# A planned attention and mixture kernel whose instruction order comes from a fixed list instead of a list scheduler, with its last product in two halves

## The chip, the cores and the metric

The kernel runs on one core of one Trainium2 chip. The metric is the time of one execution in microseconds (us), as the median of several runs. The engines are TensorE (PE in the profile; PEld is its weight load), VectorE (DVE), ScalarE (ACT), GpSimd (POOL), and SyncE (SP), which issues the transfers. Each engine takes its own instructions in the order in which the program emits them, and waits at semaphores for the others.

## The reference

```python
# attention over 4 x 8 heads: x is 512 x 64, state is 32 x 64 for each head
scores = scale * x @ state.T;   a  = exp(scores - max);  a  /= a.sum;   xread = a @ state
scores2 = scale * state @ x.T;  a2 = exp(scores2 - max); a2 /= a2.sum;  sread = a2 @ x
x = concat([xread, sread], axis=2)           # as 2176 tokens x 512
# mixture 1: 512 -> 2048 -> 512
h = x @ w_in;  g = h * tanh(softplus(h));  x = g @ w_out
# mixture 2: 512 -> 1536 -> 512, gated
xn = x / sqrt(mean(x * x) + 1e-6) * rms_g
g = xn @ w_gate;  out = (silu(g) * (xn @ w_val)) @ w_out2
```

All arrays are float32.

## The kernel before

**The work.** The tokens are cut into chunks c (512 tokens each, and a last one of the 128 rows of `sread`), the hidden width of each mixture into units u of 512. A float32 product is made of three float16 products (high by high, high by low, low by high parts), so TensorE runs nothing but short float16 matmuls in the mixtures, and VectorE and ScalarE make the two parts of every operand ("split" steps: `hi`, `l`, `s`, `join` for the weights, then `sh`, `sl`). The second mixture and the later products use seven block products in place of eight (`S1`..`S4`, `A11`, `A12`, `A22` against `T1`..`T4`, `W11`...), whose sums and differences of blocks are 128x512 steps on VectorE or ScalarE.

**Steps and their order.** The whole program is first written down as 2,476 steps: `op(engs, fn, r, w)` names the engines on which a step can run (`T` TensorE, `V` VectorE, `A` ScalarE, `D` a transfer; `X` stands for no instruction), the function that emits it, and what it reads and writes. Many elementwise steps can run on `V` or `A`. PSUM banks and SBUF tiles are taken from pools when the first step that uses one is emitted, and go back behind the last. `Plan.order` gives each step a due number from the table `RANK` and calls `Plan.forward`, a list scheduler that keeps a clock for each engine by the cost numbers of the steps and picks, whenever an engine is free, the ready step with the smallest due number; a step that can run on two engines goes where it is picked first. `Plan.run` then emits the steps in that order, and each engine's program follows from it. Steps that need another activation table on ScalarE load one first (line 369).

**Names that the prediction uses.** `fold c u` (line 1092) is the first mixture's product on the attention's own factors, in 64x32 tiles of the array; its operands come from the attention (`att`, lines 849 to 999; line 859 makes an operand of chunk c on VectorE). Line 1209 is the first mixture's input product, line 1247 its activation's last step on VectorE, line 1285 its output product, lines 1420 and 1504 the two products of the second mixture. `pow2` (line 567) is a tiny matmul that a weight's scale needs. `copy_to` (lines 553, 555 and 557) is a copy on ScalarE or, without and with a scale, on VectorE. "Stirs" (line 912) are 40 short matmuls on ones that nobody reads.

**The end.** `finish` closes a chunk of the second mixture. Three PSUM banks A, B_ and C hold partial products, `a1`, `u2` and `u3` are 512-column tiles in SBUF. `over` adds another product into a bank (`lprod`, 12 matmuls of 256 columns), `add` scales a bank and adds a tile (line 1557), `more` adds the part that earlier units left in DRAM (line 1563), and the last transfers (line 1613) write 256 KB blocks of the output. The last block product of a chunk is `A22` by `T4` into B_, followed by one `add` of 512 columns.

Of the kernel before, what the change touches and what calls it, by code (L numbers as in the profile page):

```python
# [32 lines left out]
RANK = [int(k) for k in """  # L33
# [118 lines left out]


class Plan:

    STEAL, SWITCH, MODE, BACK, STICK = 200, 0, 0.1, 0.14, 0.0

    @staticmethod
    def hop(a, b):

# [18 lines left out]
    def op(self, engs, fn, r=(), w=(), tab=None, at=None, reserve=0, lat=0.0, after=(), due=None, name="", brief=False):  # L184
# [25 lines left out]
        return o  # L210

    TICK = 10.24 / 3

    def paced(self, t, cost, busy):


# [1716 lines left out]
```

## Time and the profile before

| | us |
|---|---|
| median of 3 runs (lowest, highest) | 713.35 (713.31, 716.23) |
| profiled execution | 712.52 |
| its span in the trace | 710.6 |
| TensorE, VectorE, ScalarE busy | 697.0, 632.4, 456.5 |

The profiled execution has 1.92 us that lie outside the span; the median of the runs is 0.83 us above it. A busy share is an average over the span: the rows further down cut it into stretches.

### The profile page before, as it was taken

How to read it: one execution, taken by the hardware profiler on the slowest of the kernel's cores; microseconds unless marked ns; L12 is line 12 of the kernel's file. 1: busy time of each engine (PE TensorE's matmuls, PEld its weight loads, DVE VectorE, ACT ScalarE, POOL GpSimd, SP SyncE). 2: the span in 40 equal slices, each digit the busy share in tenths (PEclk: the TensorE clock that was granted, in tenths of full speed). 3: DMA queues.
4: the chain of work that ended last, by engine and by line, in shares of the span. 5: the costliest groups of instructions: out<-in, count | busy, mean ns of one | idle time of the engine just before them, and what ended most of it. 6: DMA issues, size and time to landing. Idle time of an engine off the chain costs nothing.

```text
span 710.6 us, 14166 instructions
## 1 busy us (share of the span) xinstructions
PE 697.0 (98%) x5818; PEld 492.2 (69%) x5818; DVE 632.4 (89%) x1147; ACT 456.5 (64%) x766; POOL 0.7 (0%) x6
## 2 busy tenths in 40 slices
PE   9999999999999999999999999999999999999997
PEld 7544444345444444457888889988888988899986
DVE  5999999999999999899999999957799486988997
ACT  6999999899987999688967466532224222513330
POOL 0000000000000000000000000000000000000000
PEclk9999999999999999999999999999999999999999
DMA  7785534246246362946400111934122263350115
GB/s 226 223 266 173 195 119 134 79 160 193 105 149 242 151 246 104 345 159 216 171 2 16 45 55 52 333 126 149 46 75 90 82 245 120 134 178 2 60 31 193
DMA packets 42084, 101.05 MB, mean 142 GB/s; under 512 B 16676, under 2 KB 18724, under 8 KB 39588
## 3 DMA queue, kind: packets, MB, share of 16 engines
q1 hardware_dynamic: 42020, 100.15, 40.7%
q8 instruction: 45, 0.74, 0.4%
q14 instruction: 19, 0.16, 0.1%
HBM read 67.90 MB, written 32.24 MB: 141 GB/s over the span
## 4 chain that ended last, share of the span: by engine, by line
PE 49%; DVE 10%; ACT 2%; DMA 1%; issue 1%; DVEq 0%; SPq 0%
PE p L1420 25%; PE a L1504 14%; PE a L1285 4%; PE p L1640 2%; DVE tt L1432 1%; DMA attm<-in_moe_w_gate_dram 1%; PE p L1217 1%; PE a L1687 1%; DVE slot L1356 1%; PE p L1209 1%; DVE rms L1383 1%; DVE slot L1392 1%; DVE tt L1471 1%; ACT junk L702 1%; DVE psm L682 1%
## 5 line engine op out<-in xcount | busy, mean ns | idle before, releaser
L1285 PE MATMUL a<-g,w2m 128*128 128x512 f16 (+1 forms) x864 | 163.7, 344 | 2.1 <-DVE g L1247 0.7
L1285 PEld LDWEIGHTS <-w2m 128*128 128x128 f16 x864 | 75.1, 98 | 83.1 <-issue 9.6
L1420 PEld LDWEIGHTS <-attm 128*128 128x128 f16 x1008 | 98.5, 98 | 14.0 <-issue 2.3
L1420 PEld LDWEIGHTS <-w 128*128 128x128 f16 x1008 | 98.5, 98 | 11.3
L1432 DVE TENSOR_TENSOR tt<-p,tt 128x512 f32<-128x512 f32 x120 | 81.9, 685 | 24.1 <-PE p L1420 23.2
L1209 PE MATMUL p<-slot,rms 128*128 128x512 f16 x336 | 77.6, 379 | 0.4 <-ACT tt L1231 0.4
L1420 PE MATMUL p<-slot,attm 128*128 128x256 f16 x576 | 68.9, 273 | 0.6 <-DVE tt L1432 0.6
L1420 PE MATMUL p<-slot,w 128*128 128x256 f16 x576 | 69.4, 273 | 0.0
L1504 PEld LDWEIGHTS <-w2m 128*128 128x128 f16 x576 | 56.2, 98 | 7.1 <-issue 0.6
L1209 PEld LDWEIGHTS <-rms 128*128 128x128 f16 x336 | 32.3, 98 | 40.1 <-issue 2.2
L553 ACT ACTIVATE g<-tt 128x512 f16<-128x512 f32 x32 | 19.2, 625 | 61.7 <-DVE tt L1471 46.5
L1456 ACT ACTIVATE tt<-tt,page 128x512 f32<-128x512 f32 x36 | 25.9, 720 | 42.8 <-DVE tt L1432 42.7
L553 ACT ACTIVATE w2m<-tt 128x512 f16<-128x512 f32 x41 | 24.9, 623 | 35.1 <-DVE tt L1471 23.2
L1504 PE MATMUL a<-attm,w2m 128*128 128x256 f16 x384 | 46.5, 273 | 0.2 <-DVE slot L1557 0.2
L1504 PEld LDWEIGHTS <-g 128*128 128x128 f16 x432 | 42.2, 98 | 4.9
L553 ACT ACTIVATE psm<-psm,page 128x512 f16<-128x512 f32 (+1 forms) x54 | 38.0, 720 | 10.8 <-DVE psm L715 9.9
L1231 ACT ACTIVATE tt<-p,page 128x512 f32<-128x512 f32 x60 | 39.9, 692 | 3.7 <-DVE g L1247 2.8
L1247 DVE SCALAR_TENSOR_TENSOR g<-tt,page,g 128x1024 f16<-128x1024 f32 (+1 forms) x32 | 38.6, 1212 | 0.8 <-ACT g L553 0.5
L1557 DVE SCALAR_TENSOR_TENSOR rms<-a,page,rms 128x512 f32<-128x512 f32 x38 | 28.2, 746 | 10.7 <-PE a L1504 9.9
L715 DVE SCALAR_TENSOR_TENSOR psm<-psm,page 128x512 f16<-128x512 f32 x49 | 36.0, 743 | 0.7
L1504 PE MATMUL a<-attm,g 128*128 128x256 f16 x288 | 35.0, 273 | 0.0
L1463 DVE TENSOR_TENSOR w2m<-tt,w2m 128x512 f16<-128x512 f32 x51 | 33.7, 681 | 0.1
(239 smaller groups left out, 1226.5 us busy)
## 6 DMA issues: line engine op xcount, KB each, us to landing
psm<-in_moe_w_out_dram SPq DMA_DIRECT2D x14, 1024.0 KB, 5.0
psm<-in_moe_w_in_dram SPq DMA_DIRECT2D x8, 1024.0 KB, 9.1
psm<-in_moe_w_val_dram SPq DMA_DIRECT2D x6, 1024.0 KB
part<-rms SPq DMA_DIRECT2D x24, 256.0 KB, 2.9
psm<-part SPq DMA_DIRECT2D x6, 1024.0 KB, 5.3
kept_wv<-psm SPq DMA_DIRECT2D x9, 512.0 KB, 2.7
kept_w<-psm SPq DMA_DIRECT2D x9, 512.0 KB
attm<-in_moe_w_gate_dram SPq DMA_DIRECT2D x4, 1024.0 KB, 6.6
```

The source lines that it names most:

```text
L553: nc.scalar.activation(o, i, ACTF.Copy, scale=1.0 if scale is None else scale)
L715: op({"V": v1(512) + 0.06}, lambda e: nc.vector.scalar_tensor_tensor(lo, f, s, h, ALU.mult, ALU.subtract), r=[*fn_, *hn, sname], w=ln, nam ...
L1209: nc.tensor.matmul(P[ph], P[folds[u][k]][:, a, f:f + 128], xh[:, k, b, :], start=(k, a, b) == (0, 0, 0), stop=(k, a, b) == (1, 1, 0))
L1231: op({"A": a_ps(512) + 0.1}, lambda e, sp=sp, i=i, ph=ph, ce=ce: nc.scalar.activation(P[sp][:, 512 * i:512 * i + 512], P[ph], ACTF.Mish, s ...
L1247: nc.vector.scalar_tensor_tensor(lo, x, rh, hi, ALU.mult, ALU.subtract)
L1285: nc.tensor.matmul(P[ya[d]][:, :n], part("wo", u, f, a)[:, d * 128:(d + 1) * 128], P[g[0]][:, g[1], b, i * n:(i + 1) * n], start=first and ...
L1420: nc.tensor.matmul(P[to][:, f * 256:f * 256 + 256], part(w, u, j, a)[:, k * 256 + f * 128:k * 256 + f * 128 + 128], h[:, k, b, :], start=b ...
L1432: op({"V": v1(512)}, lambda e: nc.vector.tensor_tensor(P[to], P[bank_], P[a], ALU.add), r=[bank_, a], w=[to], name=f"{w} add")
L1456: op({"A": a_ps(512) + 0.13}, lambda e, i=i, o=o: nc.scalar.activation(P[o], P[i], ACTF.Silu, scale=c3), r=[i, f"c3{u}"], w=[o], tab="silu ...
L1463: op({"V": v1(512)}, lambda e: nc.vector.tensor_tensor(P[g][:, 1, :], P[s], P[g][:, 0, :], ALU.subtract), r=[s], w=[g], name="gl")
L1504: nc.tensor.matmul(P[to][:, t * 256:t * 256 + 256], P[g][:, a, o:o + 128], part("w2", u, j, b)[:, f * 256:f * 256 + 256], start=begin and ...
L1557: op({"V": v1(512) + 0.06}, lambda e: nc.vector.scalar_tensor_tensor(o(), two(P[bank_]), osc, a(), ALU.mult, ALU.add), r=[bank_, *an, on_] ...
```

## The change

`order`, `forward` and their cost model are gone, and so is `RANK`. `SEQ` is a list of 2,477 numbers: step number times two, plus one where the step runs on VectorE though it could run elsewhere. `run` walks it. The cost numbers in four `op` calls differ too, but nothing reads them any more. In `finish`, the last chunk's last product is two steps of 6 matmuls, each with an `add` of 256 columns and a transfer of its own.

```diff
-RANK = [int(k) for k in """
-1863 2262 -10597 -10585 397 1959 375 -630 1862 -1285 376 1858 -1285 -774 1494 385 -3466 -4 -2115 -345 -85 175 451
...
+SEQ = [int(k) for k in """
+32 0 4 46 62 64 58 60 6 9 10 50 34 53 74 48 70 72 66 68 76 100 82 114 138 96 90 126 154 150 80 140 226 160 162 158 164
...
-        for _, o, e in self.order():
+        assert sorted(k >> 1 for k in SEQ) == list(range(len(self.ops)))
+        done = set()
+        for k in SEQ:
+            o = self.ops[k >> 1]
+            assert o.deps <= done
+            done.add(o)
+            e = "V" if k & 1 else next(x for x in o.engs if x != "V" or len(o.engs) == 1)
...
-    def lprod(to, g, u, j, begin=False):
+    def lprod(to, g, u, j, begin=False, ts=(0, 1)):
 
         def fn(e):
-            for t in range(2):
+            for t in ts:
...
-        over(B_, "A22", T4)
-        add(*c21, B_, t(a1), [a1])
-        put(a1, 1, 0)
+        if last and c == B - 1:
+            v, rd = place(1, 0)
+            op({"X": 0.01}, lambda e: None, w=[B_, (B_, 0), (B_, 1)], name="half")
+            for k in range(2):
+                lprod(B_, gs["A22"], u, T4, ts=(k,))
+                op({"V": v1(256) + 0.06}, lambda e, k=k, v=v: nc.vector.scalar_tensor_tensor(
+                    v[:, k], two(P[B_])[:, k], osc, two(P[a1])[:, k], ALU.mult, ALU.add),
+                    r=[(B_, k), B_, a1, on_], w=rd[k:k + 1], name="end add")
+        else:
+            over(B_, "A22", T4)
+            add(*c21, B_, t(a1), [a1])
+            put(a1, 1, 0)
...
-                    op({"D": 0.78}, lambda e, i=i, j=j, v=v: nc.sync.dma_start(
-                        out=out[c * R:c * R + S, :].rearrange("(p t) d -> p t d", t=4)[:, 2 * i:2 * i + 2, 256 * j:256 * j + 256],
-                        in_=v), r=rd, lat=1.9, name="out")
+                    for ks in (slice(0, 2),) if (i, j) != (1, 0) else (slice(0, 1), slice(1, 2)):
+                        o = out[c * R:c * R + S, :].rearrange("(p t) d -> p t d", t=4)[:, 2 * i:2 * i + 2, 256 * j:256 * j + 256]
+                        op({"D": 0.78 if (i, j) != (1, 0) else 0.5}, lambda e, o=o, ks=ks, v=v: nc.sync.dma_start(
+                            out=o[:, ks], in_=v[:, ks]), r=rd[ks], lat=1.9, name="out")
```

The program has the same 5,541 matmuls. ScalarE has 626 activations where it had 660, and 18 table loads where it had 21; VectorE has 1,061 steps where it had 1,026: 96 steps went from ScalarE to VectorE, 62 the other way. Every line number of the code falls by 150 to 170.

**VectorE at the program's start.** The rows stand behind the three fills that open its program; `tt_74` at line 555 takes the transposed input of the attention, `a0_89` to `a3_92` are the banks with the first scores. Before:

```order
L555 COPY tt_74<-p1_86 128x512
L555 COPY tt_74<-p0_85 128x512
L943 STREAM_TRANSPOSE attm_72<-a0_89 128x256
L943 STREAM_TRANSPOSE attm_72<-a1_90 128x256
L948 TENSOR_REDUCE page1_104<-a0_89 128x1
```

Now:

```order
L390 COPY attm_72<-attm_72 128x64
L390 COPY attm_72<-p2_87 128x256
L783 TENSOR_REDUCE page1_104<-a0_89 128x1
L783 TENSOR_REDUCE page1_104<-a1_90 128x1
L785 TENSOR_REDUCE page0_69<-page1_104 128x1
```

The two copies of the input have gone to ScalarE, two smaller copies have come in their place, and the maxima stand ahead of the transposes.

**VectorE ahead of the third chunk's attention operand.** The last row of each piece (line 859, now 694) makes the operand for which `fold c2 u0` waits. Before:

```order
L975 TENSOR_SCALAR page5_108<-page5_108 128x1
L976 RECIPROCAL page5_108<-page5_108 128x1
L659 TENSOR_SCALAR sxm_75<-psm_73 128x1024
L963 TENSOR_REDUCE page5_108<-attm_72 128x16
L964 TENSOR_SCALAR page5_108<-page5_108 128x16
L965 RECIPROCAL page5_108<-page5_108 128x16
L715 SCALAR_TENSOR_TENSOR psm_73<-psm_73,page0_69 128x512
L968 TENSOR_TENSOR attm_72<-attm_72,page5_108 128x512
L715 SCALAR_TENSOR_TENSOR psm_73<-psm_73,page0_69 128x512
L970 STREAM_TRANSPOSE tt_74<-attm_72 128x512 x2
L859 SCALAR_TENSOR_TENSOR slot2_80<-attm_72,page0_69,slot2_80 128x128
```

Now:

```order
L799 TENSOR_SCALAR page5_108<-page5_108 128x16
L800 RECIPROCAL page5_108<-page5_108 128x16
L517 SCALAR_TENSOR_TENSOR psm_73<-psm_73,xs_77 128x2x256 x2
L1082 SCALAR_TENSOR_TENSOR g_84<-tt_74,page6_109,g_84 128x2x512
L939 SCALAR_TENSOR_TENSOR rms_83<-p3_88,rms_83 128x512
L610 TENSOR_TENSOR psm_73<-psm_73 128x512
L1137 SCALAR_TENSOR_TENSOR slot0_78<-a2_91,page5_108,slot2_80 128x512
L1137 SCALAR_TENSOR_TENSOR slot0_78<-a3_92,page5_108,slot2_80 128x512
L803 TENSOR_TENSOR attm_72<-attm_72,page5_108 128x512
L694 SCALAR_TENSOR_TENSOR slot2_80<-attm_72,page0_69,slot2_80 128x128
```

The last row was the 317th of VectorE's program and is the 302nd. The split steps of the weights (line 715) that stood between the rows of the attention have gone elsewhere, and sums of the activation (lines 939 and 1082) and of the output (line 1137) stand there.

**VectorE and TensorE at the end.** `a1_90` is bank B_, `a2_91` bank C, `rms_83` holds the tiles `a1` and `u3`, and a name in brackets is the engine whose count a row waits for. VectorE's last rows before:

```order
L1557 SCALAR_TENSOR_TENSOR rms_83<-a1_90,page9_118,rms_83 128x512 [waits PE_49]
L1563 TENSOR_TENSOR rms_83<-rms_83,attm_72 128x512 [waits DVE_49]
L1563 TENSOR_TENSOR rms_83<-rms_83,attm_72 128x512
L1557 SCALAR_TENSOR_TENSOR slot3_81<-a2_91,page9_118,rms_83 128x2x256 [waits DVE_49,PE_49]
L1557 SCALAR_TENSOR_TENSOR slot3_81<-a1_90,page9_118,rms_83 128x2x256 [waits DVE_49,PE_49]
L1557 SCALAR_TENSOR_TENSOR slot3_81<-a2_91,page9_118,rms_83 128x2x256 [waits PE_49]
```

VectorE's last rows now:

```order
L1393 SCALAR_TENSOR_TENSOR rms_83<-a1_90,page9_118,rms_83 128x512 [waits PE_49]
L1399 TENSOR_TENSOR rms_83<-rms_83,attm_72 128x512 [waits DVE_49]
L1393 SCALAR_TENSOR_TENSOR slot3_81<-a2_91,page9_118,rms_83 128x2x256 [waits DVE_49,PE_49]
L1399 TENSOR_TENSOR rms_83<-rms_83,attm_72 128x512
L1445 SCALAR_TENSOR_TENSOR slot3_81<-a1_90,page9_118,rms_83 128x256 [waits DVE_49,PE_49]
L1445 SCALAR_TENSOR_TENSOR slot3_81<-a1_90,page9_118,rms_83 128x256 [waits PE_49]
L1393 SCALAR_TENSOR_TENSOR slot3_81<-a2_91,page9_118,rms_83 128x2x256 [waits PE_49]
```

And TensorE's rows now, from the last matmul of the first half of B_ to the second half and on to the first of the last product on C:

```order
L1339 MATMUL a1_90<-attm_72,w2m_71 128x256
L1339 LDWEIGHTS w2m_71
L1339 MATMUL a1_90<-attm_72,w2m_71 128x256 [waits DVE_49]
L1339 LDWEIGHTS w2m_71
L1339 MATMUL a1_90<-attm_72,w2m_71 128x256
```

The `add` from C stands ahead of the second `more`, the `add` from B_ is two of 256 columns, and TensorE's second half in B_ waits for a count of VectorE, which is reached when the first 256-column `add` has ended.

## Rows read from the trace of the kernel before

**Rows 1.** The page, part 1: busy time of each engine.

```profile
PE 697.0 (98%) x5818; PEld 492.2 (69%) x5818; DVE 632.4 (89%) x1147; ACT 456.5 (64%) x766; POOL 0.7 (0%) x6
```

**Rows 2.** Windows: stretch, length, busy time of the engines, PEclk, DMA share, GB/s.

```profile
100.00:200.00 100.00, 98.56 (x742) 45.48 (x742) 96.97 (x199) 95.63 (x164) 0.00 (x0) 1.00 0.38 128
300.00:430.00 130.00, 129.14 (x1224) 104.02 (x1224) 125.51 (x214) 92.93 (x156) 0.00 (x0) 1.00 0.28 100
430.00:700.00 270.00, 270.00 (x2617) 243.66 (x2615) 222.20 (x362) 90.34 (x147) 0.00 (x0) 1.00 0.33 115
```

**Rows 3.** Four of eighteen waits of TensorE, the two longest among them.

```profile
PE a L988 <- ACT attm L553: 1.3, 1, 1.3
PE p L873 <- ACT tt L1153: 1.2, 1, 1.2
PE a L1285 <- DVE g L1247: 0.7, 1, 0.7
PE a L1504 <- DVE slot L1557: 0.2, 1, 0.2
```

**Rows 4.** Windows of 1 us behind the idle time at 20.6 to 23.0 us.

```profile
25.00:26.00 1.00, 1.00 (x2) 0.48 (x2) 1.00 (x2) 1.00 (x2) 0.00 (x0) 0.50 0.78 175
28.00:29.00 1.00, 1.00 (x10) 0.92 (x8) 1.00 (x2) 0.51 (x2) 0.00 (x0) 1.00 0.34 70
```

**Rows 5.** Windows, cut at the start of fold c2 u0.

```profile
0.00:165.87 165.87, 157.86 (x1062) 78.99 (x1062) 151.56 (x331) 154.75 (x248) 0.70 (x6) 0.99 0.53 171
165.87:706.68 540.81, 539.13 (x4757) 413.23 (x4756) 480.06 (x816) 301.73 (x519) 0.00 (x0) 1.00 0.38 133
```

**Rows 6.** VectorE and ScalarE groups by form, busy and mean ns of one.

```profile
L775 DVE TENSOR_TENSOR psm<-psm 128x512 f32<-128x512 f32 x28 | 18.6, 680 | 0.5 <-ACT psm L553 0.5
L557 DVE TENSOR_SCALAR psm<-psm,page 128x512 f16<-128x512 f32 x9 | 4.2, 481 | 0.1
L553 ACT ACTIVATE psm<-psm,page 128x512 f16<-128x512 f32 x40 | 28.3, 718 | 10.5 <-DVE psm L715 9.9 <-DVE page L581 0.4
L369 ACT ACT_TABLE_LOAD x20 | 25.7, 1283 | 0.4
```

**Rows 7.** Waits of VectorE from 10 to 430 us, three for ScalarE.

```profile
DVE attm L715 <- ACT attm L553: 1.2, 1, 1.2
DVE psm L682 <- ACT psm L553: 1.1, 1, 1.1
DVE slot L982 <- ACT slot L553: 0.6, 1, 0.6
```

**Rows 8.** Timeline of TensorE: start, length, line, count.

```profile
114.42 2.75 PE L1285 MATMUL a<-g,w2m 128*128 128x512 f16 x12
117.11 0.84 PE L1092 MATMUL p<-w,slot 64*32 64x512 f16 x24
125.66 2.75 PE L1285 MATMUL a<-g,w2m 128*128 128x512 f16 x12
128.25 0.17 PE L567 MATMUL p<-page,ones 128*128 128x8 bf16 x1
```

**Rows 9.** Timeline of the last 9 us.

```profile
702.22 1.47 PE L1504 MATMUL a<-attm,g 128*128 128x256 f16 x12
702.42 0.75 DVE L1557 SCALAR_TENSOR_TENSOR rms<-a,page,rms 128x512 f32<-128x512 f32 x1 [0.46 <-PE a L1504]
703.20 1.29 DVE L1563 TENSOR_TENSOR rms<-rms,attm 128x512 f32<-128x512 f32 x2
703.53 1.47 PE L1504 MATMUL a<-attm,w2m 128*128 128x256 f16 x12
704.41 1.40 DVE L1557 SCALAR_TENSOR_TENSOR slot<-a,page,rms 128x512 f32<-128x512 f32 x2
705.21 1.47 PE L1504 MATMUL a<-attm,w2m 128*128 128x256 f16 x12 [0.21 <-DVE slot L1557]
```

**Rows 10.** Timeline of VectorE at 165 us.

```profile
165.50 0.31 DVE L859 SCALAR_TENSOR_TENSOR slot<-attm,page,slot 128x128 f16<-128x128 f32 x1
```

More of the change, by code (lines that the diff above doesn't have):

```diff
@@ L154 @@
 class Plan:
-    STEAL, SWITCH, MODE, BACK, STICK = 200, 0, 0.1, 0.14, 0.0
-    @staticmethod
-    def hop(a, b):
-        return 0.09 if a == b and a in 'VA' else 0.0 if a == b else 0.7 if b == "T" else 0.2 if a == "T" else 0.14
     def __init__(self, nc):
@@ L210, in op @@
         return o
-    TICK = 10.24 / 3
-    def paced(self, t, cost, busy):
-        end = t
-        while cost > 1e-9:
-            k = int(end / self.TICK + 1e-6)
-            rate = 1.0 if busy.get(k - 1, 0.0) >= 0.375 * self.TICK else 0.5
-            d = min(cost / rate, (k + 1) * self.TICK - end)
-            busy[k] = busy.get(k, 0.0) + d * rate
-            cost -= d * rate
-            end += d
-        return end - t
-    def free_for(self, o, p, bs, room, turn):
-        n = len(bs)
-        if p in self.fifo and set(turn[p][:n]) != bs:
-            return False
-        return len(room[p]) >= n + (o.reserve if p in self.urgent else 0)
@@ L234, in order @@
-    def order(self):
-        for o in self.ops:
-            for d in o.deps:
-                d.succ.append(o)
-        self.index = {o: k for k, o in enumerate(self.ops)}
-        self.using, self.turn = {}, {}
-        for o in self.ops:
-            for b in o.bufs:
-                if b not in self.using:
-                    self.turn.setdefault(self.pool_of[b], []).append(b)
-                self.using.setdefault(b, []).append(o)
-        assert len(RANK) == len(self.ops)
-        return self.forward({o: t / 10 for o, t in zip(self.ops, RANK)})[1]
@@ L250, in kind @@
-    @staticmethod
-    def kind(o):
-        return o.name[:3] if o.name[:3] in ("fol", "att") else ""
-    def forward(self, late):
-        late = dict(late)
-        todo = {o: len(o.deps) for o in self.ops}
-        ready = dict.fromkeys(self.ops, 0.0)
-        turn = {p: list(bs) for p, bs in self.turn.items()}
-        free = {e: 0.0 for o in self.ops for e in o.engs}
-        waiting = {e: [] for e in free}
-        events, out, table, n = [], [], "exp", 0
-        busy, takes, gives = {}, {}, {}
-        room = {p: [None] * max(len(t), 1) for p, t in self.pools.items()}
-        left = dict(self.users)
-        held = set()
-        front = min(o.at for o in self.ops if o.at is not None)
-        mode = None
-        for o in self.ops:
-            if not o.deps:
-                for e in o.engs:
-                    waiting[e].append(o)
-        t = 0.0
-        while True:
-            moved = True
-            while moved:
-                moved = False
-                for e in free:
-                    if free[e] > t:
-                        continue
-                    best = None
-                    for o in waiting[e]:
-                        if o in takes or ready[o] > t:
-                            continue
-                        pen = self.SWITCH if o.tab and e == "A" and o.tab != table else 0.0
-                        if e == "V" and len(o.engs) > 1:
-                            pen = self.STEAL
-                        if e == "T" and self.kind(o) != mode:
-                            pen = self.STICK
-                        key = -1.0 if o.brief else late[o] + pen, self.index[o]
-                        if best is not None and key >= best[0]:
-                            continue
-                        need = {}
-                        for b in o.bufs:
-                            if b not in held:
-                                need.setdefault(self.pool_of[b], set()).add(b)
-                        if all(self.free_for(o, p, bs, room, turn) for p, bs in need.items()):
-                            best = key, o
-                    if best is None:
-                        continue
-                    o = best[1]
-                    cost = o.engs[e]
-                    if e == "A" and o.tab and o.tab != table:
-                        table = o.tab
-                        cost += 1.28
-                    if e == "T":
-                        kind = self.kind(o)
-                        cost = self.paced(t, cost + (self.MODE if kind != mode else 0.0), busy)
-                        mode = kind
-                    takes[o] = cost
-                    if o.at is not None:
-                        front = max(front, late[o])
-                    for b in o.bufs:
-                        if b not in held:
-                            p = self.pool_of[b]
-                            held.add(b)
-                            turn[p].remove(b)
-                            giver = room[p].pop(0)
-                            if giver is not None:
-                                gives.setdefault(giver, []).append(o)
-                            if p in self.urgent:
-                                for s in self.using[b]:
-                                    late[s] = min(late[s], front)
-                    free[e] = t + cost
-                    n += 1
-                    heapq.heappush(events, (t + cost + o.lat, n, o, e))
-                    heapq.heappush(events, (t + cost, n + 0.5, None, e))
-                    out.append((t, o, e))
-                    moved = True
-                for e in waiting:
-                    waiting[e] = [o for o in waiting[e] if o not in takes]
-            if not events:
-                break
-            t = events[0][0]
-            while events and events[0][0] <= t:
-                _, _, o, e = heapq.heappop(events)
-                if o is None:
-                    continue
-                if type(o) is tuple:
-                    room[o[0]].append(o[1])
-                    continue
-                for b in o.bufs:
-                    left[b] -= 1
-                    if not left[b]:
-                        n += 1
-                        heapq.heappush(events, (t + self.BACK, n, (self.pool_of[b], o), e))
-                for s in o.succ:
-                    todo[s] -= 1
-                    ready[s] = max(ready[s], t + max(self.hop(e, x) for x in s.engs))
-                    if not todo[s]:
-                        for x in s.engs:
-                            waiting[x].append(s)
-                        if ready[s] > t:
-                            n += 1
-                            heapq.heappush(events, (ready[s], n, None, e))
-        if len(out) != len(self.ops):
-            return None
-        return max(t + takes[o] + o.lat for t, o, _ in out), out, takes, gives
@@ L566, in pow2 @@
         top = part.bitcast(BF16).rearrange("p (n w) -> p n w", w=2)[:, :, 1]
-        op({"T": 0.08}, lambda e: nc.tensor.matmul(P[b][:, :k], ones16, top, start=True, stop=True),
+        op({"T": 0.03}, lambda e: nc.tensor.matmul(P[b][:, :k], ones16, top, start=True, stop=True),
            r=pnames, w=[b], reserve=1, brief=True, name=f"pow2 {nm}")
@@ L672, in fetch @@
             for part, fn in (("l", low), ("s", sign)):
-                early_raw.append(op({"A": a_sb(1024) + 0.14, "V": v2(1024)}, fn, r=[r, q], w=[(q, part)], name=f"{part} {w}{u}{v}"))
+                early_raw.append(op({"A": a_sb(1024) + 0.38, "V": v2(1024) + 0.04}, fn, r=[r, q], w=[(q, part)], name=f"{part} {w}{u}{v}"))
             for ks in ((2 * v, 2 * v + 1),) if flat else ((2 * v,), (2 * v + 1,)):
@@ L1094, in fn @@
                             start=(a, b) == (0, 0), stop=(a, b) == (1, 0), tile_position=(64 * r, 32 * k))
-        cost = pe(512, 3)
+        cost = pe(512, 3) + 0.12
         op({"T": cost}, fn, r=[("st", c), *slotm[c].names(1024, 256), *part_names("wi", u, range(4)), *out],
@@ L1507, in fn @@
                             start=begin and (t, f, a, b) == (0, 0, 0, 0),
-                            stop=(t, f, a, b) == (1, 1, 1, 0), skip_group_check=True)
-        cost = pe(256, 12)
-        op({"T": cost}, fn, r=[g, *part_names("w2", u, [j])], w=[to], at=clock[0], name=f"l3 u{u} {j}")
+                            stop=(t, f, a, b) == (ts[-1], 1, 1, 0), skip_group_check=True)
+        cost = pe(256, 6 * len(ts))
+        op({"T": cost}, fn, r=[g, *part_names("w2", u, [j])], w=[to] if len(ts) == 2 else [(to, ts[0])], at=clock[0],
+           name=f"l3 u{u} {j}")
         clock[0] += cost
```

3 lines of the change are left out of this document (1 added, 2 removed), and 213 rows, old and new, of tables (RANK, SEQ).

## The prediction

> **What bounds the kernel now.** I read the busy shares first. TensorE works 697.0 us [rows 1] and its matmuls stay the same, so an order can only give back what TensorE loses. The windows come next, because the shares change along the span: from 430 to 700 us TensorE is busy without a break while VectorE has 48 us to spare; from 100 to 200 us it loses 1.4 us, VectorE 3.0 and ScalarE 4.4 [rows 2]. All there is to win lies ahead of 430 us, where three engines are full together. The list of TensorE's waits sizes it: 9.6 us in all with the start's 1.05; the longest two, of 1.3 and 1.2 us, end at copies on ScalarE, and ScalarE ends about 6.3 us of the eighteen, VectorE 2.2 [rows 3]. The first has a second price: behind the idle time at 20.6 to 23.0 us the granted clock is 0.50, which is 1.2 GHz, until about 27.7 us, and full at 28 [rows 4]; half speed from 24.0 to 27.7 is some 1.85 us. So 11.4 us is the ceiling of what any order can bring.
>
> **Which engine really holds TensorE back.** A wait names who came last, and that engine may have been late because of another. I add, at a TensorE piece, the VectorE work that must be done ahead of it in VectorE's order and the TensorE work that stands behind it. The end of the last matmul (706.68 us) is this sum plus VectorE's idle time ahead and TensorE's idle time behind. At `fold c2 u0`, which starts at 165.87, VectorE has worked 151.6 us and TensorE has 539.1 us to go [rows 5]: 690.7, so VectorE lost 14.3 us ahead of it and TensorE 1.7 behind. Some 8.4 of the 14.3 pass before the first scores reach VectorE at 9.8 us. A place with a larger sum has less slack.
>
> I made this sum for each TensorE piece, in both orders, with the mean durations of the groups of before (VectorE: 680 ns for a 128x512 sum, 481 for a scaled copy [rows 6]) and undisturbed TensorE pieces, which makes it 1 to 2 us smaller than the windows do:
>
> - `fold c2 u0` (165.9 us): 248 VectorE steps ahead, now 234; 153.2 us, now 143.7; TensorE behind 536.3, now 537.6. Sum 689.5, the largest of before; now 681.3.
> - `fold c0 u3` (117.1 us): 174 steps, now 165; 105.5 + 583.4 = 688.9, now 103.3 + 582.1 = 685.4.
> - an output product of the first mixture (92.5 us): 133 steps, now 127; 82.5 + 606.2 = 688.7, now 81.3 + 604.3 = 685.6.
> - the new largest, an input product of the chunk before (`l1 g2 u0`): 88 steps, now 102; 57.4 + 625.4 = 682.8, now 67.5 + 619.1 = 686.6.
> - the stretch from 340 to 430 us: 682.0 to 682.5, now 682.1 to 683.4.
>
> **The change, step by step.**
>
> *Order and engines, up to 430 us.* The largest sum falls from 689.5 to 686.6. With VectorE's idle time as it is, that is **-2.9 us**. The bounds: nothing, if each wait only moves; and at most TensorE's own waits from 30 to 430 us, 6.3 us.
>
> *ScalarE.* The steps that come to VectorE (13 us more in all) stand nearly all behind 450 us, under its 48 us of slack. ScalarE loses 17 us of work and three table loads of 1283 ns, 3.8 us of it [rows 6]; ahead of the `pow2` at 105 us, its work and TensorE's behind make 676.6 where they made 686.3. VectorE waited for ScalarE about 7 us from 10 to 430 us; the longest of those waits are 1.2, 1.1 and 0.6 us [rows 7]. I take one, of 0.6: **-0.6 us** (0 to -3).
>
> *Tile modes.* Twelve output matmuls take 2.69 us from start to start when 64x32 tiles follow (114.42 to 117.11), 2.59 when full tiles follow (125.66 to 128.25) [rows 8]: 0.10 us for a change of mode. TensorE's order changes between attention or fold pieces and the rest 65 times where it did 75 times, 6 of the 10 behind the first 120 pieces: **-0.6 us** (0, where TensorE waits anyway, to -1.0).
>
> *The start.* Two copies of 0.69 us leave VectorE's first rows, but they go to ScalarE, and the chain over both engines to the first mixture product comes out at 24.5 us instead of 24.66, with some 2 us of stirs put behind it. **0** (-1 to +1); I expect the idle time near 21 us and the half clock to stay.
>
> *Transfers.* SP now issues a write-back of the gate weights behind a weight load, at about 311 us instead of 284; it lands by 326 us at the latest by the times of the loads around it, and is needed at 331. **0.** If that cover went, each us of delay would be one on TensorE, since nothing else is ready there.
>
> *The end.* Before, VectorE ran `add` (702.42 to 703.17), two `more`, and then from 704.41 the `add` from C, for whose end the last product waited until 705.21 [rows 9]. TensorE's products follow each other in 1.31 us there (702.22 to 703.53), so it could have started at 704.84: 0.37 lost. Now the `add` from C stands ahead of the second `more`, 703.90 to 704.60, and the second `more` ends at 705.25. Only then comes the first half's `add`. Its form is not in the trace; 128x128 takes 0.31 us [rows 10] and 128x512 0.75, a line between gives 0.46 for 256 columns. So it ends at about 705.72. TensorE finished that first half at about 704.27, but the row of the second half waits for this `add`; with the 0.08 us from an `add` to the matmul behind it, as at 705.21, it starts at 705.80, and the last product 0.66 later, at 706.46 instead of 705.21: **+1.25 us**. What follows the last product is the same.
>
> The Trainium skill, page "PSUM — Partial Sum Buffer", section "PSUM bank collisions raise a hardware error", says that two engines may not touch one bank and quadrant at a time, disjoint columns included. By that rule the wait between the halves must be there, since both lie in one bank, and splitting the product costs the 1.25 us; without it the split would give the 0.37 back. The row that shows the like is the last of rows 9: a product into C waits for the `add` that reads C.
>
> **Sum:** -2.9 - 0.6 - 0.6 + 1.25 = -2.85 us against the profiled execution's 712.52, so 709.7; the median of the runs lies 0.83 above that execution, so **710.5**.
>
> **The rivals.**
>
> 1. *Waits for ScalarE were the true bound.* For it: ScalarE ended 6.3 of TensorE's 9.6 us. If these go with its lighter load, and half of the half-clock time with them, the gain is 6.3 + 0.9 - 1.25 = 5.9: **707.4**; with all of VectorE's relief counted too, about 705.5. Against it: full engines hand their lateness on, and ScalarE was as full as VectorE.
> 2. *Nothing comes of it.* Half of the pieces change places in TensorE's order; each new neighbour can bring a wait of 0.2 to 0.6 us like the eleven short ones. If waits merely move, the end's term is left: **714.6**.
> 3. *Slower: VectorE in the second mixture's first part.* From 300 to 430 us VectorE is busy 125.5 of 130 us [rows 2], and its sums there rise by up to 1 us. VectorE had lost 25.9 us by 430 us. If the new order's waits ahead make that 26 again or more, and not 24, the sum at 340 to 430 us becomes the bound: +1 there, up to +1 from the start, +1.25 at the end, **716.6**. It decides from about 26 us of VectorE's idle time at 430 us. Against it: VectorE has fewer steps in front of the early pieces, so it should reach 340 us sooner.
> 4. *The halves overlap.* If TensorE's second half did not wait for the first `add`, the end would gain 0.37 instead of losing 1.25: 1.6 less, **708.9**. Against it stands the wait in TensorE's order.
>
> **How the numbers follow.** My forecast, with its terms moved inside their bounds (708 to 712.5), has 0.46; rival 1 0.25, rival 2 0.12, rival 3 0.13, rival 4 0.04. The range reaches from rival 1's far end, 705.5, over the forecast and rival 2 up to 715; it leaves out rival 3 and a little below. A change of 0.5%, 3.57 us, is about what a measurement can tell from none: faster means below 709.8, slower above 716.9. Faster is rival 1, rival 4 and a third of the forecast, less the upper end of rival 1: 0.42. Slower is the upper half of rival 3 and what I did not think of: 0.12. The rest is 0.46.
>
> **What the profile of the changed kernel would show.** The first term: VectorE's work done ahead of `fold c2 u0` near 144 us, and fewer waits for VectorE and ScalarE between 60 and 300 us, with TensorE's idle time down from 9.6 to about 6 and the extra below. ScalarE: busy near 440 us, 17 or 18 table loads. The end: an idle time of TensorE of about 1.5 us between two halves of 6 matmuls in B_, put down to the 256-column `add`, and none ahead of the last product. The start: idle time near 21 us and a clock of 0.5 behind it. The prediction fails if waits of over 1 us appear that have no counterpart now, if the half clock vanishes or comes twice, or if the gate weights arrive late near 331 us.

## The result, and the profile after

The changed kernel takes 706.99 us (median of 4 runs, 706.45 to 707.60), the kernel before 713.33 in the same comparison (4 runs, 712.89 to 716.23): a ratio of 0.9903, 95% interval 0.9875 to 0.993. In a later comparison on one other chip the same kernel came to 707.90 against 712.97, ratio 0.9926 (0.9906 to 0.9946). The profiled execution took 707.23 with a span of 705.4; the one of before took 712.52 with a span of 710.6, so 5.3 and 5.2 us more. So the change is 5 to 6.3 us faster; the prediction said 2.85.

The page of the changed kernel, busy time of each engine, against [rows 1]:

```profile
PE 691.7 (98%) x5818; PEld 491.2 (70%) x5818; DVE 645.2 (91%) x1182; ACT 435.5 (62%) x729; POOL 0.7 (0%) x6
```

Two things stand here. TensorE is busy 5.3 us less with the same 5,541 matmuls, and that is all of the difference: its idle time did not fall (9.8 us up to its last matmul, before 9.7), though its parts did change. VectorE has 13 us more and ScalarE 21 less. The windows (stretch, length, then PE, PEld, DVE, ACT and POOL busy, PEclk, DMA share, GB/s), three that answer [rows 2], and three that cut the whole run at 30 and 430 us:

```profile
100.00:200.00 100.00, 98.81 (x737) 45.63 (x736) 96.72 (x205) 93.94 (x161) 0.00 (x0) 1.00 0.39 127
300.00:430.00 130.00, 129.63 (x1280) 108.25 (x1279) 127.72 (x225) 94.04 (x160) 0.00 (x0) 1.00 0.36 127
430.00:700.00 270.00, 268.06 (x2583) 241.17 (x2581) 234.02 (x382) 70.51 (x115) 0.00 (x0) 1.00 0.35 121
0.00:30.00 30.00, 25.30 (x221) 18.17 (x222) 21.06 (x55) 22.24 (x37) 0.70 (x6) 1.00 0.73 219
30.00:430.00 400.00, 396.84 (x3009) 230.78 (x3008) 388.89 (x745) 342.76 (x579) 0.00 (x0) 1.00 0.45 152
430.00:701.46 271.46, 269.51 (x2594) 242.23 (x2591) 234.50 (x383) 70.51 (x115) 0.00 (x0) 1.00 0.35 122
```

And the same three last stretches of the kernel before:

```profile
0.00:30.00 30.00, 26.91 (x233) 20.32 (x234) 20.65 (x52) 22.31 (x37) 0.70 (x6) 0.94 0.76 229
30.00:430.00 400.00, 393.61 (x2916) 222.84 (x2915) 383.49 (x726) 343.82 (x584) 0.00 (x0) 1.00 0.44 152
430.00:706.68 276.68, 276.47 (x2673) 249.06 (x2670) 227.49 (x369) 90.34 (x147) 0.00 (x0) 1.00 0.34 119
```

TensorE's idle time from 30 to 430 us went from 6.39 to 3.16 us. Ahead of 30 us it rose from 3.09 to 4.70, but there the mean granted clock was 0.94 before and is 1.00 now. Behind 430 us it rose from 0.21 to 1.95. Six of the twelve waits of the changed kernel, against [rows 3] (line waited at, who released it, us in total, times, longest):

```profile
PE a L1339 <- DVE slot L1445: 1.6, 1, 1.6
PE a L823 <- ACT attm L388: 1.4, 1, 1.4
PE a L754 <- DVE attm L392: 1.1, 1, 1.1
PE p L834 <- ACT rms L388: 0.7, 1, 0.7
PE p L1255 <- ACT rms L1170: 0.4, 1, 0.4
PE a L1120 <- DVE g L1082: 0.4, 1, 0.4
```

The first is the second half of the split product, and the second stands ahead of 30 us. Of the listed waits from 30 to 430 us ScalarE ended 4.4 us before and ends 1.5 now; VectorE ended 1.7 before and ends 1.5 now. The windows of [rows 4]:

```profile
25.00:26.00 1.00, 1.00 (x5) 0.52 (x4) 1.00 (x2) 1.00 (x2) 0.00 (x0) 1.00 0.94 214
28.00:29.00 1.00, 1.00 (x4) 0.52 (x3) 1.00 (x3) 1.00 (x1) 0.00 (x0) 1.00 0.00 0
```

The half clock at 25 us is not there. The cut at `fold c2 u0`, which answers [rows 5]:

```profile
0.00:158.27 158.27, 152.04 (x1057) 77.46 (x1057) 146.13 (x323) 148.36 (x241) 0.70 (x6) 1.00 0.56 179
158.27:701.46 543.19, 539.62 (x4763) 413.71 (x4762) 498.31 (x859) 287.15 (x489) 0.00 (x0) 1.00 0.38 133
```

That piece starts 7.6 us sooner. VectorE has done 146.1 us of work ahead of it (151.6 before), and has lost 12.1 (14.3). The end of the program, against [rows 9] and [rows 10] (start, length, engine, line, and in brackets the idle time ahead and who ended it):

```profile
696.87 0.82 PE L1339 MATMUL a<-attm,w2m 128*128 128x256 f16 x6
698.01 0.68 DVE L1399 TENSOR_TENSOR rms<-rms,attm 128x512 f32<-128x512 f32 x1
698.80 0.48 DVE L1445 SCALAR_TENSOR_TENSOR slot<-a,page,rms 128x256 f32<-128x256 f32 x1
699.33 2.12 PE L1339 MATMUL a<-attm,w2m 128*128 128x256 f16 x18 [1.65 <-DVE slot L1445]
700.18 0.48 DVE L1445 SCALAR_TENSOR_TENSOR slot<-a,page,rms 128x256 f32<-128x256 f32 x1 [0.91 <-PE a L1339]
701.50 0.75 DVE L1393 SCALAR_TENSOR_TENSOR slot<-a,page,rms 128x512 f32<-128x512 f32 x1 [0.83 <-PE a L1339]
```

TensorE runs 6 matmuls, waits 1.65 us for the 256-column `add` (0.48 us), and then runs the other 6 and the last product without a break.

### The profile page after: what moved, and what is told of

Its sections match the earlier page's. It is cut to its first block, busy times and chain, and to the rows that moved or that the text cites. A ratio compares the mean times of both kernels' runs of the same rounds, so it can differ in the third digit from the quotient of the medians.

```text
span 705.4 us, 14169 instructions
## 1 busy us (share of the span) xinstructions
PE 691.7 (98%) x5818; PEld 491.2 (70%) x5818; DVE 645.2 (91%) x1182; ACT 435.5 (62%) x729; POOL 0.7 (0%) x6
## 4 chain that ended last, share of the span: by engine, by line
PE 75%; DVE 19%; ACT 3%; DMA 2%; issue 1%; SPq 0%; DVEq 0%; ACTq 0%
PE p L1255 28%; PE a L1120 14%; PE a L1339 13%; PE p L1044 6%; PE a L1002 4%; PE p L978 2%; PE p L1486 2%; DVE g L1082 2%; PE p L1052 2%; DVE psm L550 1%; DVE slot L1137 1%; PE a L1533 1%; DVE rms L939 1%; DVE slot L1393 1%; DMA attm<-in_moe_w_gate_dram 1%
## 5 line engine op out<-in xcount | busy, mean ns | idle before, releaser
L388 ACT ACTIVATE w2m<-tt 128x512 f16<-128x512 f32 x34 | 21.0, 623 | 67.2 <-DVE tt L1306 27.1
L388 ACT ACTIVATE psm<-psm,page 128x512 f16<-128x512 f32 (+1 forms) x46 | 32.5, 717 | 6.7 <-DVE psm L550 5.2
L1317 DVE TENSOR_TENSOR tt<-tt 128x512 f32<-128x512 f32 x48 | 32.7, 687 | 0.7
```

The costliest lines, as they stand in the source:

```text
L388: nc.scalar.activation(o, i, ACTF.Copy, scale=1.0 if scale is None else scale)
L1317: op({"V": v1(512)}, lambda e: nc.vector.tensor_tensor(P[o], P[a], P[b], f), r=[a, b], w=[o], name="gsum")
```

## The experiments

OLD and NEW stand for the two lists of steps in the order in which the two kernels emit them. In all but e5 the last product into B_ is whole. Each kernel is compared with the kernel before on the chip that it ran on; chips differ by up to 1.5 us in the median of the kernel before (711.8 to 713.3), so between comparisons only ratios and traces are set side by side.

**e1 and e6: the last product whole again.**

```diff
-        if last and c == B - 1:
-            v, rd = place(1, 0)
...
-        else:
-            over(B_, "A22", T4)
-            add(*c21, B_, t(a1), [a1])
-            put(a1, 1, 0)
+        over(B_, "A22", T4)
+        add(*c21, B_, t(a1), [a1])
+        put(a1, 1, 0)
```

> The changed kernel's list with the last product into B_ whole again (one product of 12 matmuls, one add of 512 columns, one transfer). Theory that the second half's wait for the first half's add is all loss: TensorE's idle time of 1.65 us between the halves goes, the last matmul ends 1.3 to 1.5 us sooner, and the median comes to 705.5 (705.2 to 706.0) where the change has 707.0. Rival, that the halves pay for the wait with a shorter add and an earlier transfer at the end: 707.0 within 0.3.

> The changed kernel unedited, beside the next two on one chip, since the kernel with the whole last product ran on another chip than the changed one. Both theories: a ratio to the kernel before of 0.990 (0.987 to 0.993).

> The changed list with the last product into B_ whole, once more. Its last matmul ended 0.6 us sooner in spite of a start that was 0.55 us later and a wait that was 0.64 longer, but its span ran on for 4.85 us behind the last add, where the changed kernel's ran 3.17. Theory that the output transfers set the end (the 1 MB of the chunk before, the small packets of the last chunk and the last blocks lie on each other), so that the split only moves TensorE's time under them: equal to the changed kernel within 0.5 us, and again more than 4.5 us from the last add to the end. Rival, that the first run's tail was chance: 1.3 to 1.8 us below the changed kernel on the same chip.

e1 gave 708.51 (6 runs, ratio 0.9936, 0.9917 to 0.9955), which none of its theories had. So e5, the changed kernel, and e6, the whole product once more, ran side by side: 707.90 (0.9926, 0.9906 to 0.9946) and 707.73 (0.9922, 0.9903 to 0.9941). No difference: the split's 1.65 us on TensorE are not in the time. The end of e6 shows why. TensorE, VectorE and the queue of SP:

```profile
696.82 2.78 PE L1339 MATMUL a<-attm,w2m 128*128 128x256 f16 x24
698.07 3.08 SPq L1451 DMA_DIRECT2D out_dram<-slot  x3
698.75 1.65 DVE L1393 SCALAR_TENSOR_TENSOR slot<-a,page,rms 128x512 f32<-128x512 f32 x2
```

The last add ends at 700.40, and the span ends at 705.3, 4.9 us later. In the changed kernel the last add ends at 702.25, and only 3.2 us pass to 705.4. The windows of e6 behind 699 us:

```profile
699.00:701.00 2.00, 0.60 (x6) 0.29 (x3) 1.25 (x2) 0.00 (x0) 0.00 (x0) 1.00 0.99 386
701.00:703.00 2.00, 0.00 (x0) 0.00 (x0) 0.00 (x0) 0.00 (x0) 0.00 (x0) 1.00 0.88 308
```

The transfer engines are 0.99 and 0.88 busy while the computing engines stop. So in the new list the output transfers set the end, and a TensorE that is done sooner waits for them.

**e7: the last chunk's output sooner.** The new list issues the output of the 128-row chunk and the 1 MB of the chunk before right behind each other, at 693.8 and 695.3 us.

```diff
-SEQ = NEW
+SEQ = [k for k in NEW if k not in (4930, 4932)]   # the last chunk's add and its transfer
+at = SEQ.index(4926) + 1                          # right behind the sum that they need
+SEQ[at:at] = [4930, 4932]
```

> As e6, but the last chunk's add and its transfer (the one of 32-row pieces, in small packets) stand in the list right behind the sum that the add needs, some 4 us sooner, so that it is through before the 1 MB transfer of the chunk before starts. Theory that the transfers set the end: the span ends about 3.1 us behind the last add as in the kernel before, 1.3 to 1.8 us below e6, which makes it the fastest, 705.3 to 706. Rival, that the 1 MB and the last blocks alone fill the queues: no change against e6.

707.21 us (6 runs; ratio 0.9921, 0.9902 to 0.994), by its median not to be told from e5 and e6. The traces tell more, since two things vary from run to run and can be taken off. The first is the opening, whose 28 matmuls took 4.77 us in the changed kernel and 6.14 here:

```profile
1.05 4.77 PE L1665 MATMUL a<-ones 128*128 128x256 f16 x28 [1.05 <-DVE ones L1670]
5.67 1.06 PE L708 MATMUL p<-ident,attm 128*128 128x128 f32 x8
```

```profile
1.05 6.14 PE L1656 MATMUL a<-ones 128*128 128x256 f16 x28 [1.05 <-DVE ones L1661]
7.00 0.74 PE L708 MATMUL p<-ident,attm 128*128 128x128 f32 x5
...
126.19 2.10 PE L1120 MATMUL a<-g,w2m 128*128 128x512 f16 x9 [0.27 <-ACT slot L388]
```

The output product at 124.82 in the changed kernel starts at 126.19 here, 1.37 later, and the opening's difference is 1.37 by its length and 1.33 by the matmul behind it: it goes through one to one. The same product, in the changed kernel:

```profile
124.82 2.75 PE L1120 MATMUL a<-g,w2m 128*128 128x512 f16 x12 [0.22 <-ACT slot L388]
```

The second is a weight load near 222 us. VectorE's waits for it, in e5 and in e11 (the changed kernel has 0.7 us, e6 0.3):

```profile
DVE xs L503 <- DMA attm<-in_moe_w_gate_dram: 1.9, 1, 1.9
```

```profile
DVE xs L503 <- DMA attm<-in_moe_w_gate_dram: 3.5, 1, 3.5
```

TensorE waits behind it at 230 us: 0.36 us in the changed kernel, 1.00 in e1, 1.67 in e5, 3.14 in e11, not at all in e6, e7 and e10. With both taken off, the span is:

| one trace each | span | start of the matmul behind the opening | wait at 230 us | span less both |
|---|---|---|---|---|
| changed kernel, split | 705.4 | 5.67 | 0.36 | 699.4 |
| e5, split | 706.7 | 5.75 | 1.67 | 699.3 |
| e1, whole | 706.5 | 6.28 | 1.00 | 699.2 |
| e6, whole | 705.3 | 5.87 | 0 | 699.4 |
| e7, whole, early transfer | 705.2 | 7.00 | 0 | 698.2 |

By this reckoning split and whole are equal to 0.2 us, and the early transfer is worth 1.1. The medians don't show the 1.1: the ratios of e6 and e7 are 0.9922 and 0.9921. The last adds of e7 end at 701.48, and its span ends 3.7 us later:

```profile
699.83 1.65 DVE L1393 SCALAR_TENSOR_TENSOR slot<-a,page,rms 128x512 f32<-128x512 f32 x2
```

**e9 and e10: a shorter opening, and the third chunk's output in halves.**

```diff
-ROUSE, STIRS = 28, 40
+ROUSE, STIRS = 21, 40
...
-        for i in range(2) if c == 0 else [None]:
+        for i in range(2) if c in (0, 2) else [None]:
```

> As e7, with 21 matmuls on ones at the program's opening instead of 28. In five profiles of the new order the 28 take 4.8 to 6.1 us, with the same matmuls, and all of TensorE's work behind starts later by as much; the first input lands at 5.3 to 5.5 us. Theory that the opening goes into the end one to one, since TensorE hardly waits between 38 and 124 us: the transposes start at about 5.4 us, the median falls by 0.3 to 1.0 against e7, to 706.2 to 706.9, and the runs spread less. Rival, that VectorE's and ScalarE's sums hold the later pieces: no change against e7 (707.2). Second rival, that the granted clock now stays at half into the transposes: up to 1 us slower.

> As e9, and the 1 MB output transfer of the third chunk is two of 512 KB, the first issued some 3 us before the second, when its two quarters are done. Theory that the transfers set the end: the span ends 3.1 to 3.3 us behind the last add (e7 3.7), 0.4 to 0.7 us below e9. Rival: what is left behind the last add is one block's own time, no change.

e9, with the first line alone, gave 706.98 (6 runs; ratio 0.9936, 0.9911 to 0.996), e10 706.87 (6 runs; 0.9926, 0.991 to 0.9943); the kernel before had 711.8 on this chip. The transposes started at 5.59 us in both. By the ratios no gain over the changed kernel is shown. The traces, by the same reckoning, give 698.9 (706.0 - 5.59 - 1.51) and 698.5 (704.1 - 5.59); both hold a wait of 0.63 us at 155 us that is 0.10 in the changed kernel, and e9 another of 0.28 at 8.2. Both have e7's early transfer too, and both lie below the 699.2 to 699.4 of the lists without it. The span of e10 ended 3.9 us behind the last add: the halves bought nothing, against their theory.

**e2 and e12: one list up to 130 us, then the other.**

```diff
-SEQ = NEW
+SEQ = NEW[:574] + [k for k in OLD if k >> 1 not in {j >> 1 for j in NEW[:574]}]   # e2
+SEQ = OLD[:565] + [k for k in NEW if k >> 1 not in {j >> 1 for j in OLD[:565]}]   # e12
```

> The changed kernel's order and engines up to the step that TensorE reached at 130 us (574 steps), then the rest in the order and on the engines of before, last product whole. By then the changed kernel leads by about 5 us of TensorE's time. Theory of the largest sum (VectorE's work ahead plus TensorE's work behind, with VectorE's idle time as it is): the sum at fold c2 u0 is 686.7 by the medians of both traces, as high as the largest of before (686.4), so the lead is lost again by 166 us and the time is 712.5 to 714. Rival, that time won on TensorE stays won: 708 to 709.

> The opposite of e2: the order and engines of before up to the step that TensorE reached at 130 us, then the changed kernel's, last product whole. The changed kernel led by 5.0 us at 130 us and by 7.4 at 430. Theory that a list's later part needs the earlier part's state (e2's wait of 5.1 us at the seam): the largest sum ahead of 130 us is that of before (686.4), new waits at the seam: 712 to 716. Rival, that each stretch has its own worth: 713 less 2.4, 710 to 711.

e2 gave 714.04 (12 runs; ratio 1.0025, 1.001 to 1.004): the lead of 5 us is gone, as the sum had it, though not at `fold c2 u0` but at once. TensorE stands still for 5.1 us at the seam, for VectorE, which is busy all the time: the wait, and VectorE's window over it (length, busy, PEclk, DMA share, GB/s):

```profile
140.95 1.44 PE L1120 MATMUL a<-g,w2m 128*128 128x512 f16 x3 [5.10 <-DVE slot L1137]
```

```profile
125.00:140.90 15.90, 15.44 (x37) 1.00 0.21 83
```

The steps that the old list had given to VectorE early were still ahead of what TensorE needed. Behind this wait the granted clock was 0.50 for about 3.4 us, some 1.7 us more:

```profile
142.00:143.00 1.00, 1.00 (x3) 0.29 (x2) 0.78 (x2) 0.73 (x2) 0.00 (x0) 0.50 0.81 291
```

e12 gave 712.73 (12 runs; 1.0006, 0.9994 to 1.0018): behind the old list's beginning the later part of the new list wins nothing. Its TensorE ended 1.4 us sooner than before (705.25), and its span 5.6 us behind that, with the new list's crowded end. A seam between two lists brings waits of its own, so neither run prices a stretch of the new list by itself.

**e3 and e4: the order of one with the engines of the other.**

```diff
-SEQ = NEW
+SEQ = [k & ~1 | on_v_in_OLD[k >> 1] for k in NEW]   # e3
+SEQ = [k & ~1 | on_v_in_NEW[k >> 1] for k in OLD]   # e4
```

> The changed kernel's order of all steps, but each elementwise step on the engine that it had before (158 of them differ); last product whole. By VectorE's largest sum (682.4, the new engines give 684.0) it should be 1 to 2 us faster than the changed list with the product whole: 704 to 705. By ScalarE's largest sum (683.5, the new engines give 680.4) it should be 3 us slower: about 708.5. If orders and engines only work as the pair that was tuned, new waits put it above 711.

> The order of before, but each elementwise step on the engine that the changed kernel gives it; last product whole. By VectorE's largest sum (687.8, before 686.4): 714 to 715. By ScalarE's (684.0, before 686.7): 710 to 711. If orders and engines only work as a pair: above 716.

759.72 us (4 runs; ratio 1.0659, 1.0637 to 1.068) and 739.46 us (6 runs; 1.0372, 1.0347 to 1.0398). Both of the sums fail here by 25 to 55 us, and only the rival holds: an order and its engines are one thing. In e3's trace (mean granted clock 0.981) the clock also falls to 0.50 six times ahead of 370 us, some 27 us together, which is up to 14 us that no sum counts. In e3 from 100 to 200 us no engine is full:

```profile
100.00:200.00 100.00, 90.58 (x578) 40.41 (x577) 85.85 (x169) 81.19 (x130) 0.00 (x0) 0.97 0.36 116
```

TensorE is idle 9.4 us, VectorE 14 and ScalarE 19: each stands in its own row and waits for a step that is late in another's. Two of TensorE's waits in e4 are of the same kind, one for each of the other engines, the first for the sums on ScalarE that a weight's scale needs:

```profile
PE p L402 <- ACT junk L537: 4.2, 1, 4.2
PE p L1255 <- DVE tt L390: 2.7, 3, 1.1
```

**e8 and e11: stirs later in the old list, earlier in the new.**

```diff
-SEQ = OLD
+SEQ = OLD with its last 6 stirs ahead of the second group of transposes   # e8
-SEQ = NEW
+SEQ = NEW with the 8 stirs of 16.9 to 25 us ahead of the first group      # e11
```

> The order and engines of before; only 6 of its 40 stirs, which ran at about 18 us, stand ahead of the second group of transposes, in TensorE's idle time at 21.7 to 23.0 us. Theory on the clock: TensorE is not idle there and the granted clock stays 1.00 from 24 to 28 us. For the time there are two theories: that VectorE and ScalarE set the place of the waits at 63 to 93 us, so the 1.9 us won at 28 us go into longer waits there: 713.3 within 0.7 of the kernel before; or that TensorE's time won at the start stays won: 1.5 to 2 us below the kernel before.

> The changed list with the whole last product, but the eight stirs that stand between 16.9 and 25 us go ahead of that, to the others at 10 to 16 us. Theory on the clock: TensorE is idle for some 3 us between 17 and 24 us, and the granted clock falls to 0.5 behind it, from about 24 to 28 us, as in the kernel before; since TensorE has no idle time from 38 to 124 us in this order, the 1.5 to 2 us come out at the end: 709.2 to 709.7 where e6 had 707.7. Rival: the clock falls but the time is taken back out of VectorE's slack, or it does not fall: 707.7 within 0.5.

e8 gave 713.68 (12 runs; 1.0005, 0.9989 to 1.0021). It didn't remove the idle time, which moved ahead of and between the stirs, and the clock fell as before, so its theory on the clock was not put to the test. Its windows at 20 and behind 24 us:

```profile
20.00:21.00 1.00, 0.12 (x4) 0.00 (x0) 0.93 (x4) 1.00 (x5) 0.00 (x0) 1.00 0.99 393
24.00:25.00 1.00, 1.00 (x6) 1.00 (x6) 0.93 (x5) 1.00 (x2) 0.00 (x0) 0.50 0.81 179
25.00:26.00 1.00, 1.00 (x7) 1.00 (x6) 0.93 (x2) 1.00 (x2) 0.00 (x0) 0.50 0.69 155
```

e11 gave 708.36 (11 runs; 0.9949, 0.9933 to 0.9965), 0.3% above e6's ratio with intervals that touch; its trace, 700.5 by the reckoning above (710.5 - 6.91 - 3.14), is 1.0 above e6. The clock did not fall at 24 us, though TensorE had idle times of 0.75, 0.48 and 0.84 us from 20 to 24.6; it fell behind the wait of 3.14 us at 231, from about 235.5 to 238.9 us. Half speed over 3.4 us is some 1.7 us, more than the 1.0. The windows at 23, 25 and 236 us:

```profile
23.00:24.00 1.00, 0.26 (x9) 0.10 (x1) 0.90 (x6) 1.00 (x4) 0.00 (x0) 1.00 1.02 412
25.00:26.00 1.00, 1.00 (x4) 0.38 (x2) 1.00 (x4) 1.00 (x2) 0.00 (x0) 1.00 0.95 185
236.00:237.00 1.00, 1.00 (x3) 0.29 (x2) 0.96 (x2) 0.97 (x5) 0.00 (x0) 0.50 1.00 414
```

And in e12, whose steps up to 130 us are the old list's own, it did not fall either, behind the same two idle times, which were longer here (0.97 and 1.30 us against 0.47 and 1.29):

```profile
22.00:23.00 1.00, 0.18 (x3) 0.00 (x1) 0.97 (x4) 1.00 (x2) 0.00 (x0) 1.00 1.06 333
25.00:26.00 1.00, 1.00 (x3) 0.52 (x4) 0.98 (x3) 1.00 (x2) 0.00 (x0) 1.00 0.78 172
```

So the half clock at 24 us that the trace of before shows does not follow from its list alone. The mean granted clock of every run says the same: a fall like this one, some 1.7 us lost of 710.6, takes 0.0024 off the mean of a run, and of the 56 runs of the kernel before in the three later comparisons 29 have a mean of 0.998 or less, the other 27 of 0.999 or 1.000. In two comparisons the median of the runs with 0.998 or less lies 1.9 us above that of the others (713.2 and 711.3, 714.3 and 712.3), in the third 0.2 below (711.8 and 711.9). All 10 runs of the changed kernel (e5 among them) have 0.999 or 1.000. A mean does not tell where the clock fell. So the new list may make the fall rarer; no run shows what in it would do so. What decides the fall stays open.

## Why the prediction was right, and where it was short

**The time lies in the range, at its lower end, and the gain is about twice the 2.85 us forecast.** Of the rivals the first came nearest in time (707.4). The whole, up to TensorE's last matmul, in the profiled executions: -3.2 from 30 to 430 us, -2.3 of busy time that is neither opening nor clock, -1.4 at the start, +1.7 at the end, together -5.2 us; the forecast's terms were -3.5, -0.6, 0 and +1.25.

**The relief up to 430 us** (-2.9 and -0.6, together -3.5): TensorE's idle time from 30 to 430 us fell by 3.23 us. The size was right. The working was right in part only. At the five places for which I took it from the traces, the largest sum fell by 3.4 us, from 691.3 (at 117 us, VectorE 104.2 and TensorE 587.1) to 687.9 (at 76 us, 66.3 and 621.5), where 2.9 was forecast; but TensorE is busy without a break from 39 to 124 us, so it did not wait at the place of the new largest sum, and that the size agrees is in part luck. The sum of VectorE's work ahead and TensorE's behind did fall at `fold c2 u0` (by 8.2 as counted ahead, by 4.9 in the traces, 690.7 to 685.8), and e2 fits such a debt of VectorE, since its lead was lost again at 141 us in a wait for VectorE's late steps. But I held VectorE's idle time constant, and it fell as well: 14.3 to 12.1 us ahead of `fold c2 u0`, 25.9 to 19.9 ahead of some 425 to 430 us. And e3 and e4 show that the sums are only a lower bound: they were nearly the same there, and the time was 25 to 55 us longer than they gave. Most of all, the shares are open: I gave VectorE 2.9 and ScalarE 0.6, but by who ended them the waits that went are ScalarE's (4.4 to 1.5 us), as rival 1 had it, and VectorE's stayed (1.7 to 1.5). The engine that ends a wait may be late because of another, and e3 and e4, which were to part the two, broke the order instead. VectorE's own waits for ScalarE from 10 to 430 us fell from 6.7 to 3.6 us, and how much of its idle time went with ScalarE's lighter load was not tried.

**Tile modes** (-0.6): TensorE's busy time fell by 5.3 us. Of that the opening is 1.33 and the half clock some 1.7 (0.50 from about 24.1 to 27.5 us; the prediction read it to 27.7 and made it 1.85), which leaves 2.3. Ten changes of mode at 0.10 us would be 1.0 of it, by the prediction's price; no run changed the modes alone. The other 1.3 us is not explained.

**The start** (0): the term that failed in this pair of traces. I expected the half clock to stay, and it went; the opening was 1.33 us shorter, and TensorE's idle time ahead of 30 us 1.61 longer, together -1.4. The vanished half clock was one of the prediction's own signs of failing, and so was a new wait of over 1 us (1.1 at line 754, which was 919 and had none); both came. That the shorter opening comes from the change is not shown: its matmuls are the same, and it takes 4.8 to 6.1 us in the traces of the new list and 5.4 to 6.1 in those of the old. Whether the half clock went by the change or by chance is open (e11 and e12). The rows of its 28 matmuls in the kernel before:

```profile
1.05 6.10 PE L1819 MATMUL a<-ones 128*128 128x256 f16 x28 [1.05 <-DVE ones L1824]
```

How far such time counts in the old list is open as well. In one pair of traces it hardly does: e12 had a shorter opening by 0.7 us and no half clock, some 2.4 us together, and stood only 0.40 us ahead at 63.78, behind a wait for ScalarE; first e12, then the kernel before:

```profile
63.78 0.66 PE L708 MATMUL p<-ident,attm 128*128 128x128 f32 x4 [1.09 <-ACT tt L988]
```

```profile
64.18 0.66 PE L873 MATMUL p<-ident,attm 128*128 128x128 f32 x4 [1.18 <-ACT tt L1153]
```

But the 1.9 us between the runs of the kernel before with and without a fallen mean clock, in two comparisons of three, speak for it. In the new list TensorE is not idle between 39 and 124 us, and the opening comes through one to one (e1, e7).

**Transfers in the middle** (0): no wait at the gate weights' write-back. But the load at 222 us, which the prediction did not name, costs TensorE 0 to 3.1 us from trace to trace in the new list.

**The end** (+1.25): the second half waited 1.65 us, where I had 1.53, for the `add` that I had named: rival 4 is out. What the Trainium skill says of two engines on one bank (page "PSUM — Partial Sum Buffer", section "PSUM bank collisions raise a hardware error") agrees with this wait of 1.65 us; the wait stands in the program's order, and no run leaves it out. "What follows the last product is the same" held for the changed kernel (3.9 us from the last matmul to the end in both), but the +1.25 was put down to the wrong thing. With the product whole, 4.9 us pass from the last add to the end and not 3.1, so the split's wait costs nothing that e5 and e6 show, and the end costs about as much as I had said for another reason: the outputs of two chunks lie on each other. TensorE's lead of 6.7 us at 690 us, by the pieces then left to do, was 5.2 us in the span.

**Not slower in the second mixture** (rival 3): VectorE's idle time by 425 us was 19.9, far from the 26 that it needed. **Nothing comes of it** (rival 2) is out too.

The program of before has 2,473 steps; the 2,476 in the section on it is a slip.

## What to carry to other kernels

Add, at each piece of the engine that bounds, the work that another engine must do ahead of it and its own work behind: the largest sum is a lower bound of the time and a hint where won time may be lost again, no more (it missed by 25 to 55 us in e3 and e4), and here the order and its choice of engines were worth nothing apart. Before a last product is cut up, see what follows the last instruction: here the output transfers of two chunks set the end, and moving one of them by 4 us was worth 1.1 us in the traces, though not in the medians, where the cut was worth nothing. A difference of 1% between two traces can hold several us of chance (an opening, a clock, one load): take these off by the rows before the change is given the credit, and look at the mean clock of every run and not of the profiled one alone.

## What the runs showed of the hardware that was not expected

The 28 matmuls of the opening took 4.8 to 6.1 us from trace to trace at the same place, the changed kernel's 4.77 and 4.87 and the same list with the product whole 4.98 and 5.39. The Trainium skill, page "TensorE: Matmul & The Clock Gate", section "Part 1: The HAM clock gate (the "warmup" mystery)", says that the number of matmuls that run at the lower clock at a kernel's start changes from run to run of one kernel; the spread of these rows agrees, but the lower clock itself is not in them: the granted clock reads 1.00 in every window of these openings, while 7 of the matmuls stand in the window at 4 us in the kernel before and 10 in the changed one:

```profile
4.00:5.00 1.00, 1.00 (x7) 0.73 (x5) 0.00 (x0) 0.00 (x0) 0.00 (x0) 1.00 1.09 383
4.00:5.00 1.00, 1.00 (x10) 0.85 (x8) 0.00 (x0) 0.00 (x0) 0.00 (x0) 1.00 1.06 365
```

One 1 MB weight load near 222 us, in the same list, held VectorE for 0.3 us in e6 and for 0.7 and 1.9 in the two traces of the changed kernel; in e11, whose list differs at the start alone, for 3.5. The granted clock fell to 0.50 near 24 us behind idle times of 1.8 us together (the kernel before) and 1.9 (e8), and not behind 2.3 (e12); it fell behind single waits of 5.10 us (e2) and 3.14 us (e11).
